# Loading the last K ahead of the last four V, and a new tail for the last batch, in a cached grouped-query attention kernel

## The chip, the cores and the metric

The kernel runs on one core of one Trainium2 chip. The metric is device time in microseconds (us), the median of several executions; it is about 2 us longer than the span of the profiled execution. A ratio is the mean time of one kernel's fast runs over the mean of the other's fast runs of the same rounds, so it is not quite the ratio of the medians that are quoted.

## The reference, cut to what matters

```python
B, Sq, D = 32, 4, 1024
Hq, Hkv, Sk, Dh = 32, 4, 2048, 128
q = (x @ wq).reshape(B, Sq, Hq, Dh).transpose(0, 2, 1, 3)
k = repeat(k_cache, 8, axis=1);  v = repeat(v_cache, 8, axis=1)   # 4 KV heads serve 32 heads
p = softmax(einsum("bhqd,bhkd->bhqk", q, k) * Dh**-0.5)
o = einsum("bhqk,bhkd->bhqd", p, v)
return o.transpose(0, 2, 1, 3).reshape(B, Sq, Hq * Dh) @ wo
```

Everything is bfloat16. Each of the 32 batches reads 2 MB of K and 2 MB of V, 134 of the 151 MB that the kernel reads. The 32 heads times 4 queries of one batch fill the 128 partitions of a score tile.

## The kernel before

The programmer places every instruction on its engine, in order, with semaphore waits. Below, `slot` hands out one of four buffers in a ring in PSUM, the memory into which this kernel's matmuls write. Names like `("pv", i)` are events. P is the exponent of the scores, P^T its transpose, o is P*V; "copied" or "evicted" means moved from PSUM to SBUF, where the kernel keeps K, V and P.

```python
def load_v(b):                       # V buffer b % 3 is free once P*V of batch b-3 is done
    ...                              # the last V comes as four loads of 512 KB, one per KV head
load_k(0); load_k(1)
for b in range(B):                   # all on one DMA queue: K2 V0 K3 V1 ... K30 V28 K31 V29 V30 V31
    if b + 2 < B:
        load_k(b + 2)
    load_v(b)
...
for i in range(B):
    pe_qk(i)                         # scores of batch i into PSUM
    softmax_max(i)                   # vector engine: one max over 2048, then the bias
    if i >= 2: pe_ot(i - 2); ot_evac(i - 2)
    if i + 1 < B:                    # transposes of K(i+1), evicted by vector and scalar engine
        for f in (0, 1): pe_fill(i + 1, f); evac(i + 1, f)
    softmax_exp(i)                   # scalar engine: P and its row sums
    if i + 1 < B:
        for f in range(2, NFILL): pe_fill(i + 1, f); evac(i + 1, f)
    softmax_rinv(i)
    if i >= 1:
        pe_pv(i - 1)                 # needs V(i-1); on the tensor engine it precedes the scores of i+1
        o_evac(i - 1)                # o / row sum
    for f in range(2): pe_pt(i, f); evac_pt(i, f)   # P^T
# ... (cut) last batch L = 31: P*V of KV heads 0-2, then of head 3; o scaled, transposed and
# copied in two parts; 128 projection matmuls; copy; output DMA
```

"P*V 28" below is `pe_pv(28)`, "scores 31" is `pe_qk(31)`, and so on.

## Time and profile before

| | before |
|---|---|
| time, median of 3 | 387.33 us (387.23 to 387.41) |
| span of the profiled execution | 385.4 us |
| one 2 MB load in the steady loop | one per 5.0 us |
| first K31 transpose / scores 31 / first P^T 31 / end of span | 358.61 / 366.13 / 371.85 / 385.4 us |

The page of the kernel before, its DMA slices and the shares of the chain that ended last:

```profile
DMA  7999999999999999999999999999999999999930
...
DMA 59%; PE 17%; ACT 13%; DVE 7%; issue 2%; SPq 1%
```

The DMA engines are busy to within two slices of the end (395 to 432 GB/s in each slice from the second to the 37th), and the chain is K loads for 59% of the span. So for most of the run nothing but bytes counts. Only the tail can change. This is its timeline (start, duration, engine, line and operation, tiles, shapes, count, then idle time and releaser, which is what ended that idle time). L207 transposes K, L240 makes scores, L248 is P*V, L225 transposes P, L296 is the projection. The first line is P*V 28, and L240 comes first for batch 30, then for 31:

```profile
354.08 1.08 PE L248 MATMUL ps_r<-V_sb,PT_sb 128*32 128x128 bf16 x64 [0.92 <-ACT KT_sb L219]
...
356.09 1.05 PE L240 MATMUL ps_s<-KT_sb,QT_sb 128*32 128x512 bf16 x16
...
358.61 2.41 PE L207 MATMUL ps_r<-ident,K_sb 128*128 128x128 bf16 x40 [1.31 <-DMA K_sb<-in_k_cache_dram]
...
364.12 1.08 PE L248 MATMUL ps_r<-V_sb,PT_sb 128*32 128x128 bf16 x64 [0.93 <-ACT KT_sb L219]
...
366.13 1.05 PE L240 MATMUL ps_s<-KT_sb,QT_sb 128*32 128x512 bf16 x16
...
367.23 2.29 DVE L280 TENSOR_REDUCE mx<-ps_s 128x1 f32<-128x2048 f32 x1 [0.15 <-PE ps_s L240]
...
369.74 1.97 ACT L285 ACTIVATE P_sb<-ps_s,negmx 128x2048 bf16<-128x2048 f32 x1 [2.09 <-DVE negmx L281]
...
371.85 1.89 PE L225 MATMUL ps_r<-ident,P_sb 128*128 128x128 bf16 x16 [1.43 <-ACT P_sb L285]
...
374.53 3.16 PE L248 MATMUL ps_r<-V_sb,PT_sb 128*32 128x128 bf16 x64 [0.68 <-DVE PT_sb L231]
...
378.18 2.80 PE L296 MATMUL ps_s<-w_sb,oT_sb 128*32 128x256 bf16 x96 [0.30 <-DVE oT_sb L364]
...
382.47 0.42 DVE L309 CAST y_sb<-ps_s 128x256 bf16<-128x256 f32 x1 [1.16 <-PE ps_s L296]
```

Read it as a chain: K31 lands (358.6), 7.5 us later come scores 31, and 19.3 us after their start the kernel ends. V31 is no part of it: its last part lands at 373.9, and P^T 31 is copied only at 374.5.

The same kernel in stretches (busy time and count of each engine, granted clock of the tensor engine, DMA share, GB/s):

```profile
367.50:370.90 3.40, 1.29 (x64) 0.97 (x64) 2.17 (x2) 1.31 (x2) 0.00 (x0) 1.00 0.51 202
370.90:377.70 6.80, 5.17 (x82) 4.71 (x82) 1.55 (x3) 1.80 (x5) 0.00 (x0) 0.50 0.17 58
```

The tensor engine worked 1.3 of 3.4 us, and in the next 6.8 us its clock was half. The DMA share is 0.5 while data is still to come. The trace has the time of each of a load's 16 completions, and they come in two halves: for V30 the eighth and the ninth are 5.7 us apart, the first and the last 9.5 us. The slow half decides when a load has landed. Landings, which I took from the trace's completions (last of 16, from the span's start):

```
        K30     then            V29     V30     V31 by KV head
before  348.5   V28 353.6  K31 358.6  363.7  368.6  370.1 371.4 372.6 373.9
after   348.4   K31 353.5  V28 358.6  363.6  368.6  369.9 371.1 372.4 373.7
```

### The profile page before, as it was taken

To read this page: it belongs to the slowest core of one execution; us is meant where nothing else is said; L and a number is where in the kernel's file an instruction comes from. 1 tells how busy PE (TensorE), PEld (TensorE's weight loads), DVE (VectorE), ACT (ScalarE), POOL (GpSimd) and SP (SyncE) were. 2 spreads that over 40 slices of the span, in tenths; PEclk is the share of its full clock that TensorE was granted. 3 is DMA by queue.
4 is the path that set the end of the run, shared out by engine and by line. 5 is a ranking of instruction groups with operands and counts; after the bars stand their busy time and mean duration, and the time that the engine had idled before them with its cause. 6 is when DMAs were issued, how large, how long until landed. Compare 5 with 4: busy or idle time off the path is not lost.

```text
span 385.4 us, 12595 instructions
## 1 busy us (share of the span) xinstructions
PE 280.9 (73%) x5929; PEld 229.5 (60%) x5929; DVE 274.1 (71%) x299; ACT 208.5 (54%) x261; POOL 0.7 (0%) x6
## 2 busy tenths in 40 slices
PE   1876888676383967888767778877767888776756
PEld 1875766465282856666655566665645676565545
DVE  0017999683552984899888859998868859987850
ACT  1005777355161646676666627766646566666620
POOL 0000000000000000000000000000000000000000
PEclk9998999886976899999999999999999999999978
DMA  7999999999999999999999999999999999999930
GB/s 328 432 432 416 418 417 398 413 410 395 413 409 409 419 416 414 419 413 418 417 419 417 417 414 417 416 416 411 417 417 417 418 420 415 417 418 410 375 143 9
DMA packets 27251, 152.32 MB, mean 395 GB/s; under 512 B 1472, under 2 KB 1984, under 8 KB 22592
## 3 DMA queue, kind: packets, MB, share of 16 engines
q1 hardware_dynamic: 27104, 151.49, 96.1%
q8 instruction: 46, 0.75, 0.8%
q10 hardware_dynamic: 96, 0.03, 0.0%
q14 instruction: 5, 0.04, 0.0%
HBM read 151.26 MB, written 0.26 MB: 393 GB/s over the span
## 4 chain that ended last, share of the span: by engine, by line
DMA 59%; PE 17%; ACT 13%; DVE 7%; issue 2%; SPq 1%
DMA K_sb<-in_k_cache_dram 59%; ACT KT_sb L219 7%; ACT P_sb L285 6%; DVE KT_sb L217 4%; PE ps_r L207 4%; PE ps_r L248 3%; PE ps_r L296 3%; PE ps_r L225 3%; PE ps_s L240 3%; DVE mx L280 2%; PE ps_s L296 1%; DVE PT_sb L231 0%; SPq L129 0%; PE ps_r L271 0%; ACT oT_sb L275 0%
## 5 line engine op out<-in xcount | busy, mean ns | idle before, releaser
L207 PE MATMUL ps_r<-ident,K_sb 128*128 128x128 bf16 x2048 | 142.6, 229 | 66.0 <-DMA K_sb<-in_k_cache_dram 40.8
L217 DVE COPY KT_sb<-ps_r 128x1024 bf16<-128x1024 bf16 x128 | 148.0, 1216 | 40.0 <-PE ps_r L207 39.8
L207 PEld LDWEIGHTS ps_r<-ident,K_sb 128*128 128x128 bf16 x2048 | 125.7, 103 | 82.2 <-DMA K_sb<-in_k_cache_dram 41.9
L219 ACT ACTIVATE KT_sb<-ps_r 128x1024 bf16<-128x1024 bf16 x128 | 124.5, 1025 | 72.1 <-PE ps_r L207 72.0
L280 DVE TENSOR_REDUCE mx<-ps_s 128x1 f32<-128x2048 f32 x32 | 73.3, 2292 | 7.1 <-PE ps_s L240 4.6
L285 ACT ACTIVATE P_sb<-ps_s,negmx 128x2048 bf16<-128x2048 f32 x32 | 63.0, 1969 | 2.2 <-DVE negmx L281 2.1
L231 DVE COPY PT_sb<-ps_r 128x1024 bf16<-128x1024 bf16 x64 | 41.4, 686 | 16.7 <-PE ps_r L225 15.2
L248 PE MATMUL ps_r<-V_sb,PT_sb 128*32 128x128 bf16 x2048 | 36.7, 223 | 17.2 <-ACT KT_sb L219 12.8
L248 PEld LDWEIGHTS ps_r<-V_sb,PT_sb 128*32 128x32 bf16 x2048 | 31.0, 98 | 22.7 <-ACT KT_sb L219 19.4
L275 ACT ACTIVATE oT_sb<-ps_r 128x128 bf16<-128x128 bf16 x31 | 8.6, 277 | 55.6 <-PE ps_r L271 55.6
L225 PE MATMUL ps_r<-ident,P_sb 128*128 128x128 bf16 x512 | 35.1, 223 | 1.8 <-ACT P_sb L285 1.4
L240 PE MATMUL ps_s<-KT_sb,QT_sb 128*32 128x512 bf16 x512 | 34.3, 386 | 2.5 <-DVE KT_sb L217 1.7
L225 PEld LDWEIGHTS ps_r<-ident,P_sb 128*128 128x128 bf16 x512 | 29.4, 99 | 5.4 <-ACT P_sb L285 1.6
L240 PEld LDWEIGHTS ps_s<-KT_sb,QT_sb 128*32 128x32 bf16 x512 | 10.8, 96 | 13.3 <-issue 2.8
L187 DVE CAST QT_sb<-ps_r 128x512 bf16<-128x512 f32 x2 | 1.3, 686 | 22.4 <-PE ps_r L176 22.4
L265 ACT ACTIVATE o_sb<-ps_r,rinv 128x128 bf16<-128x128 f32 x31 | 11.4, 367 | 9.8 <-PE ps_r L248 9.8
L189 ACT ACTIVATE QT_sb<-ps_r 128x512 bf16<-128x512 f32 x2 | 1.1, 594 | 26.0 <-PE ps_r L176 26.0
L176 PE MATMUL ps_s<-P_sb,w_sb 128*128 128x128 bf16 x128 | 9.4, 232 | 7.2 <-DMA w_sb<-in_wq_dram 7.2
L296 PE MATMUL ps_r<-w_sb,oT_sb 128*32 128x256 bf16 x384 | 11.5, 273 | 2.6 <-issue 1.4
L176 PEld LDWEIGHTS ps_s<-P_sb,w_sb 128*128 128x128 bf16 x128 | 8.3, 105 | 7.8 <-issue 4.4
L296 PEld LDWEIGHTS ps_r<-w_sb,oT_sb 128*32 128x32 bf16 x384 | 10.0, 97 | 3.7 <-issue 2.5
L271 PEld LDWEIGHTS ps_r<-ident,o_sb 128*128 128x128 bf16 x31 | 3.0, 98 | 12.7 <-issue 12.7
(30 smaller groups left out, 58.9 us busy)
## 6 DMA issues: line engine op xcount, KB each, us to landing
K_sb<-in_k_cache_dram SPq DMA_DIRECT2D x32, 2048.0 KB, 25.4
V_sb<-in_v_cache_dram SPq DMA_DIRECT2D x31, 2048.0 KB, 27.3
w_sb<-in_wq_dram SPq DMA_DIRECT2D x4, 2048.0 KB, 14.8
w_sb<-in_wo_dram SPq DMA_DIRECT2D x4, 2048.0 KB, 24.7
V_sb<-in_v_cache_dram SPq DMA_DIRECT2D x4, 512.0 KB, 15.8
P_sb<-in_x_dram SPq DMA_DIRECT2D x1, 256.0 KB, 2.8
out_dram<-y_sb SPq DMA_DIRECT2D x14, 16.0 KB, 12.1
out_dram<-y_sb ACTq DMA_DIRECT2D x2, 16.0 KB, 1.6
```

Of the source, the lines that this page charges most:

```text
L176: p.op("pe", lambda e, kt=kt, h=h: e.matmul(ps_q(h), lhsT=w_sb[:, kt, h * Dh:(h + 1) * Dh], rhs=xT_sb[:, kt, :], start=(kt == 0 and h % 4 ...
L207: p.op("pe", lambda e, q=q, t=t: e.transpose(buf[:, q * 128:(q + 1) * 128], K_sb[:, b % NKB, t, :], ident[:, :]), waits + [("k", b), "iden ...
L217: p.op("dve", lambda e: e.tensor_copy(dst, src), waits, ("kt", b, f))
L219: p.op("act", lambda e: e.activation(dst, src, ACT.Copy), waits, ("kt", b, f))
L225: p.op("pe", lambda e, q=q: e.transpose(buf[:, q * 128:(q + 1) * 128], P_sb[:, (8 * f + q) * 128:(8 * f + q + 1) * 128], ident[:, :]), wai ...
L231: p.op("dve", lambda e: e.tensor_copy(PT_sb[:, 8 * f:8 * f + 8, :].rearrange("p t q -> p (t q)"), buf), [("ptf", i, f)] + ([("pv", i - 1)] ...
L240: p.op("pe", lambda e, c=c, g=g: e.matmul(ps_s[32 * g:32 * (g + 1), c * 512:(c + 1) * 512], lhsT=QT_sb[:, i, REP * g:REP * (g + 1), :], rh ...
L248: p.op("pe", lambda e: e.matmul(buf[32 * g:32 * (g + 1), 0:Dh], lhsT=PT_sb[:, t, 32 * g:32 * (g + 1)], rhs=V_sb[:, i % NVB, g, t, :], star ...
L265: p.op("act", lambda e: e.activation(o_sb[:, :], buf[:, 0:Dh], ACT.Copy, scale=rinv[:, i:i + 1]), [("pv", i), ("rinv", i)] + ([("oT", i - ...
L280: p.op("dve", lambda e: e.tensor_reduce(mx[:, i:i + 1], ps_s[:, :], AX.X, ALU.max), [("qk", i)], ("mx", i))
L285: p.op("act", lambda e: e.activation(P_sb[:, :], ps_s[:, :], ACT.Exp, bias=negmx[:, i:i + 1], scale=scale, accum_out=ssum[:, i:i + 1]), [( ...
L296: p.op("pe", lambda e, h=h, j=j: e.matmul(buf[32 * j:32 * (j + 1), 0:NC], lhsT=oT_sb[:, h, 32 * n:32 * (n + 1)], rhs=wo_sb[:, h, NC * j:NC ...
```

## The change

The intent is to have K of the last batch early, so that its softmax is done while the last V still arrive, and then to follow V31 closely, KV head by KV head. K31 is read in 4 KB rows, so that its transposed copy is contiguous. The last max is taken in four chunks, the last exponent in two. P is normalised before it is transposed, so P*V can give o^T directly, with V as the stationary operand, and the transposes of o vanish.

```diff
 def load_k(b):
+    if b < B - 1: ...                                     # as before, 16 KB rows
+    else: src = k_cache[b].rearrange("g (p t) d -> p g (t d)", p=128)   # 4 KB rows
 for b in range(B):
-    if b + 2 < B:
+    if b + 2 < B - 1:
         load_k(b + 2)
+    if b == B - 4:
+        load_k(B - 1)               # K30 K31 V28 V29 V30 V31
     load_v(b)
 def evac(b, f):
-    if f in DVE_FILLS:
+    if f in (DVE_FILLS if b < B - 1 else (2, 3, 4, 6, 7)):
@@ last batch, cut to its core
+pe_qk(L)
+for c in range(4): mxc[c] = max(ps_s[:, c*512:(c+1)*512])          # vector engine
+mx, negmx from mxc
+pe_ot(L - 2); ot_evac(L - 2)
+for k in range(2): P[k] = exp(...), accum_out=ssum[B + k]          # scalar engine
+pe_pv(L - 1)
+ssum[L] = ssum[B] + ssum[B + 1]; softmax_rinv(L)
+for f in range(2): P[f] *= rinv (vector engine); pe_pt(L, f)
+for f in range(2): evac_pt(L, f)
+o_evac(L - 1); pe_ot(L - 1); ot_evac(L - 1)
-(P*V of heads 0-2, then 3; o scaled in two parts, transposed, copied; projection of 24 + 8 heads)
+pv_last(0)                          # 16 matmuls, lhsT = V, rhs = P^T: o^T of one KV head
+for g in range(4):
+    if g + 1 < 4: pv_last(g + 1)
+    oproj_last(g)                   # 32 projection matmuls of that head group
```

The order of the tensor engine in the loop is untouched: P*V 28 still precedes the P^T of batch 29, scores 30 and the transposes of K31.

More of the change, by code (lines that the diff above doesn't have):

```diff
@@ L111, in bass_standalone__gqa_block_cached__sampling_kernel @@
         negmx = sbuf("negmx", [128, B], F32)
-        ssum = sbuf("ssum", [128, B], F32)
+        mxc = sbuf("mxc", [128, 4], F32)
+        ssum = sbuf("ssum", [128, B + 2], F32)
         rinv = sbuf("rinv", [128, B], F32)
@@ L132, in load_k @@
         def load_k(b):
-            p.dma("sp", lambda e: e.dma_start(
-                K_sb[:, b % NKB, :, :], k_cache[b].rearrange("g (r t) d -> (g r) t d", r=R)),
+            if b < B - 1:
+                dst, src = K_sb[:, b % NKB, :, :], k_cache[b].rearrange("g (r t) d -> (g r) t d", r=R)
+            else:
+                dst = K_sb[:, b % NKB, :, :].rearrange("p (g t) d -> p g (t d)", g=G)
+                src = k_cache[b].rearrange("g (p t) d -> p g (t d)", p=128)
+            p.dma("sp", lambda e: e.dma_start(dst, src),
                 [("fill", b - NKB, NFILL - 1)] if b >= NKB else [], ("k", b), f"s_k{b % NKB}")
@@ L204, in pe_fill @@
             for q in range(TB):
-                c, v = q // (TB // C), q % (TB // C)
-                t = c * TV + f * TB // C + v
+                if b < B - 1:
+                    c, v = q // (TB // C), q % (TB // C)
+                    t = c * TV + f * TB // C + v
+                else:
+                    v, g = q // G, q % G
+                    t = g * TV + f * TB // G + v
                 p.op("pe", lambda e, q=q, t=t: e.transpose(
@@ L215, in evac @@
             src = buf.rearrange("p (c m r) -> p m r c", c=C, r=R)
-            if f in DVE_FILLS:
+            if b == B - 1:
+                dst, src = KT_sb[:, f * TB // C:(f + 1) * TB // C, :, :].rearrange("p v g m -> p (v g m)"), buf
+            if f in (DVE_FILLS if b < B - 1 else (2, 3, 4, 6, 7)):
                 p.op("dve", lambda e: e.tensor_copy(dst, src), waits, ("kt", b, f))
@@ L219, in evac, with pe_pt @@
                 p.op("act", lambda e: e.activation(dst, src, ACT.Copy), waits, ("kt", b, f))
-        def pe_pt(i, f):
+        def pe_pt(i, f, ready=None):
             buf, waits = slot(("pt", i, f))
@@ L226, in pe_pt @@
                     buf[:, q * 128:(q + 1) * 128], P_sb[:, (8 * f + q) * 128:(8 * f + q + 1) * 128], ident[:, :]),
-                    waits + [("exp", i)] if q == 0 else [], ("ptf", i, f) if q == 7 else None)
+                    waits + [ready or ("exp", i)] if q == 0 else [], ("ptf", i, f) if q == 7 else None)
         def evac_pt(i, f):
@@ L244, in pe_qk @@
                         start=True, stop=True, tile_position=(0, 32 * g)),
-                        waits, ("qk", i) if (c, g) == (3, G - 1) else None)
+                        waits, (("qk", i) if c == 3 else ("qkc", i, c)) if g == G - 1 else None)
         def pv_mm(buf, i, g, t, waits, done):
@@ L319, in bass_standalone__gqa_block_cached__sampling_kernel @@
             evac(0, f)
-        for i in range(B):
+        for i in range(B - 1):
             pe_qk(i)
@@ L346, in bass_standalone__gqa_block_cached__sampling_kernel @@
         L = B - 1
+        pe_qk(L)
+        for c in range(4):
+            p.op("dve", lambda e, c=c: e.tensor_reduce(
+                mxc[:, c:c + 1], ps_s[:, c * 512:(c + 1) * 512], AX.X, ALU.max),
+                [("qkc", L, c) if c < 3 else ("qk", L)], ("mxc", c))
+        p.op("dve", lambda e: e.tensor_reduce(mx[:, L:L + 1], mxc[:, :], AX.X, ALU.max), [("mxc", 3)], ("mx", L))
+        p.op("dve", lambda e: e.tensor_scalar(negmx[:, L:L + 1], mx[:, L:L + 1], -scale, None, op0=ALU.mult),
+             [("mx", L)], ("negmx", L))
@@ new lines, in bass_standalone__gqa_block_cached__sampling_kernel @@
+        pe_ot(L - 2)
+        ot_evac(L - 2)
+        for k in range(2):
+            p.op("act", lambda e, k=k: e.activation(
+                P_sb[:, k * 1024:(k + 1) * 1024], ps_s[:, k * 1024:(k + 1) * 1024], ACT.Exp,
+                bias=negmx[:, L:L + 1], scale=scale, accum_out=ssum[:, B + k:B + k + 1]),
+                [("negmx", L), ("ptf", L - 1, 1)], ("expk", k))
+        pe_pv(L - 1)
+        p.op("dve", lambda e: e.tensor_tensor(
+            ssum[:, L:L + 1], ssum[:, B:B + 1], ssum[:, B + 1:B + 2], op=ALU.add), [("expk", 1)], ("exp", L))
@@ L347, in bass_standalone__gqa_block_cached__sampling_kernel @@
+        softmax_rinv(L)
+        for f in range(2):
+            p.op("dve", lambda e, f=f: e.tensor_scalar(
+                P_sb[:, f * 1024:(f + 1) * 1024], P_sb[:, f * 1024:(f + 1) * 1024], rinv[:, L:L + 1], None, op0=ALU.mult),
+                [("rinv", L)], ("pn", f))
+            pe_pt(L, f, ("pn", f))
+        for f in range(2):
+            evac_pt(L, f)
+        o_evac(L - 1)
         pe_ot(L - 1)
         ot_evac(L - 1)
-        o_l, waits = slot(None)
-        waits = waits + [("pt", L, 0), ("pt", L, 1)]
@@ L351, in bass_standalone__gqa_block_cached__sampling_kernel @@
-        for t in range(TV):
-            for g in range(3):
-                pv_mm(o_l, L, g, t, waits + [("v", L, k) for k in range(3)] if t == 0 and g == 0 else [],
-                      ("pva", L) if (t, g) == (TV - 1, 2) else None)
-        for t in range(TV):
-            pv_mm(o_l, L, 3, t, [("v", L, 3)] if t == 0 else [], ("pv", L) if t == TV - 1 else None)
-        p.op("act", lambda e: e.activation(o_sb[0:96, :], o_l[0:96, 0:Dh], ACT.Copy, scale=rinv[0:96, L:L + 1]),
-             [("pva", L), ("rinv", L), ("oT", L - 1)], "oa")
@@ L359, in bass_standalone__gqa_block_cached__sampling_kernel @@
-        p.op("act", lambda e: e.activation(o_sb[96:128, :], o_l[96:128, 0:Dh], ACT.Copy, scale=rinv[96:128, L:L + 1]),
-             [("pv", L)], "ob")
-        ta, waits = slot(None)
-        ta = ta.bitcast(BF16)
-        p.op("pe", lambda e: e.transpose(ta[:, 0:96], o_sb[0:96, :], ident[0:96, 0:96]), waits + ["oa"], "oTa")
-        p.op("dve", lambda e: e.tensor_copy(
-            oT_sb[:, 0:24, L * Sq:(L + 1) * Sq], ta[:, 0:96].rearrange("p (h s) -> p h s", s=Sq)), ["oTa"], "ota")
         y_l = ps_s[:, 0:512]
@@ L367, in bass_standalone__gqa_block_cached__sampling_kernel, with pv_last @@
         n = NOG - 1
-        oproj_mm(y_l, n, range(24), ["ota", ("ot", L - 1)], None)
-        tb, waits = slot(None)
-        tb = tb.bitcast(BF16)
-        p.op("pe", lambda e: e.transpose(tb[:, 0:32], o_sb[96:128, :], ident[96:128, 96:128]), waits + ["ob"], "oTb")
-        p.op("dve", lambda e: e.tensor_copy(
-            oT_sb[:, 24:32, L * Sq:(L + 1) * Sq], tb[:, 0:32].rearrange("p (h s) -> p h s", s=Sq)), ["oTb"], "otb")
-        oproj_mm(y_l, n, range(24, 32), ["otb"], ("op", n))
+        def pv_last(g):
+            buf, waits = slot(None)
+            for t in range(TV):
+                p.op("pe", lambda e, t=t: e.matmul(
+                    buf[:, 0:32], lhsT=V_sb[:, L % NVB, g, t, :], rhs=PT_sb[:, t, 32 * g:32 * (g + 1)],
+                    start=(t == 0), stop=(t == TV - 1)),
+                    waits + [("v", L, g), ("pt", L, 0), ("pt", L, 1)] if t == 0 else [],
+                    ("pvl", g) if t == TV - 1 else None)
+            p.op("dve", lambda e: e.tensor_copy(
+                oT_sb[:, 8 * g:8 * (g + 1), L * Sq:(L + 1) * Sq], buf[:, 0:32].rearrange("p (h s) -> p h s", s=Sq)),
+                [("pvl", g)], ("otl", g))
@@ L375, in bass_standalone__gqa_block_cached__sampling_kernel, with oproj_last @@
+        def oproj_last(g):
+            oproj_mm(y_l, n, range(8 * g, 8 * (g + 1)), [("otl", g), ("ot", L - 1), ("exp", L)],
+                     ("op", n) if g == G - 1 else None)
+        pv_last(0)
+        for g in range(G):
+            if g + 1 < G:
+                pv_last(g + 1)
+            oproj_last(g)
         oproj_evac(y_l, n)
```

## The prediction

> **What bounds the kernel.** The slices of the page show DMA at 9 tenths almost to the end and about 417 GB/s; the chain of waits is 59% K loads. From the landings in the trace, one 2 MB load lands every 5.0 us: K30 348.5, V28 353.6, K31 358.6, V29 363.7, V30 368.6, the four parts of V31 at 370.1, 371.4, 372.6, 373.9 us of a 385.4 us span. Half of each load's 16 completions come up to 10 us before the other half (the windows after 364 us show a DMA share of 0.5), so the slow half sets every landing and stays backlogged; a later issue does not delay it. [...]
>
> The steady loop is DMA-bound: the early iterations, whose K was already there, took 8.65 us from score matmul to score matmul, against 10.0 us of data. So only the tail after 353 us can change. There, by the chain: K31 lands 358.6, scores of batch 31 begin 366.1, max 367.2 to 369.5, exponent to 371.8, transposes to 373.8 and P*V at half clock to 377.7, projection to 382.5, end 385.4. V31 (373.9) is hardly waited for.
>
> **What the change does.** Bytes are unchanged. K31 lands one place earlier (353.6), but V28 takes its place: 358.6 in place of 353.6. P*V of batch 28 began at 354.1 before. On the tensor engine it stands, in order, ahead of scores 30 and of the transposes of K31; so the early K31 cannot be used before V28 lands. Tensor engine idle from 353.2 to 358.6.
>
> New walk, with traced durations: P*V 28 from 358.6, 1.08 us, transposes 1.0, scores 30 1.0: 361.7 with a full clock. After 5.4 us idle I expect half clock ([...] here the clock was 0.5 from 370.9 to 377.8 after a nearly idle window, and 64 P*V took 3.16 in place of 1.08 us, 16 transposes 1.89 in place of 1.07). That adds about 3 us: scores 30 end near 365. Batch 31's K eviction is cheaper (1216 to about 690 ns each on the vector engine, as the equally shaped P^T copies): about 0.9 us off the 7.65 us from scores to scores. Scores 31 begin near 371.7 (368.5 if no throttle) against 366.1.
>
> Tail from there: four max chunks, estimated 0.69 us each from the 2048- and 256-column operations, run after the P^T copies: no gain on 2.29 us. Two exponents with accumulator reads 2.4 against 2.07 us; sum, reciprocal and normalisation about 0.7 more on the path. P^T starts 7.3 us after scores against 5.7, again after about 5 us idle, so at half clock. Then 64 P*V matmuls with full-width V weights (about 62 ns each, 118 throttled) replace 64 small ones, the transposes of o vanish, and 128 projection matmuls stay: about 9 us against 8. Output 2.5 us as before. Tail about 22.5 us against 19.3.
>
> Sum: 3 to 6 us later scores, 3 us longer tail: +6 to +9 us, nearly all on the critical path.
>
> **Predicted: 394.5 us**, range 390.5 to 398. Faster by over 2%: 0.02; within 2%: 0.54; slower by over 2%: 0.44.
>
> **What the profile would show.** P*V 28 waiting on DMA of V for about 4.5 us; clock 0.5 near 357 to 364 and again near 378; scores 31 later than 366; no wait for V31; data ending near 374; eviction near 690 ns.
>
> **What would make it wrong.** No throttle in either gap (then about 390); a slow normalisation; a different skew of the DMA halves on that chip; V28 landing early enough to hide its delay.

The sum: 3 to 6 us later scores and a tail longer by 3 us, +6 to +9 us, and a point of 394.5 us. The half clock is the estimate from one measured stretch, 370.9 to 377.7 us of the kernel before. That a later issue does not delay a landing was an inference, and the changed kernel bears it out: V28 was issued at 334.11 us, 1.19 us later than K31 before, and landed at 358.60 against 358.56; the parts of V31 were issued 3.9 to 5.5 us later than before and landed 0.24 to 0.27 us earlier. The 2.4 us for two exponents and the 0.7 us for sum, reciprocal and normalisation are estimates; the changed kernel took 2.31 us (374.29 to 376.60) and 0.91 us (376.60 to 377.51).

## The result, and the profile after

The changed kernel takes 391.99 us (391.98 to 392.75, 3 runs) against 387.33 us; ratio 1.0127, 95% interval 1.0104 to 1.015. That is slower, but within 2%. Its timeline (L261 is P*V, L238 the transposes of P, L253 scores, L218 transposes of K, L362 the max chunks, L371 the exponents, L380 the normalisation, L395 the last P*V, L309 the projection):

```profile
358.73 1.90 PE L261 MATMUL ps_r<-V_sb,PT_sb 128*32 128x128 bf16 x64 [4.93 <-DMA V_sb<-in_v_cache_dram]
...
360.56 1.89 PE L238 MATMUL ps_r<-ident,P_sb 128*128 128x128 bf16 x16
...
362.38 1.56 PE L253 MATMUL ps_s<-KT_sb,QT_sb 128*32 128x512 bf16 x16
...
363.94 2.40 PE L218 MATMUL ps_r<-ident,K_sb 128*128 128x128 bf16 x40
...
368.32 1.08 PE L261 MATMUL ps_r<-V_sb,PT_sb 128*32 128x128 bf16 x64
...
370.53 1.05 PE L253 MATMUL ps_s<-KT_sb,QT_sb 128*32 128x512 bf16 x16
371.40 2.47 DVE L362 TENSOR_REDUCE mxc<-ps_s 128x1 f32<-128x512 f32 x4
...
374.29 1.11 ACT L371 ACTIVATE P_sb<-ps_s,negmx 128x1024 bf16<-128x1024 f32 x1 [2.23 <-DVE negmx L366]
...
377.01 0.88 DVE L380 TENSOR_SCALAR P_sb<-P_sb,rinv 128x1024 bf16<-128x1024 bf16 x2
...
377.56 1.89 PE L238 MATMUL ps_r<-ident,P_sb 128*128 128x128 bf16 x16 [3.00 <-DVE P_sb L380]
...
380.32 1.02 PE L395 MATMUL ps_r<-PT_sb,V_sb 128*128 128x32 bf16 x32 [0.77 <-DVE PT_sb L244]
...
381.27 1.90 PE L309 MATMUL ps_s<-w_sb,oT_sb 128*32 128x256 bf16 x32
...
385.25 1.93 PE L309 MATMUL ps_s<-w_sb,oT_sb 128*32 128x256 bf16 x64
...
387.23 0.42 DVE L322 CAST y_sb<-ps_s 128x256 bf16<-128x256 f32 x1 [1.69 <-PE ps_s L309]
```

P*V 28 begins at 358.73, 0.13 us after V28 landed, where it began at 354.08 before. The waits of the stretch from 353 us on name the releaser (waiter, releaser, total us, times, longest), and the stretches show the clock:

```profile
PE ps_r L261 <- DMA V_sb<-in_v_cache_dram: 4.9, 1, 4.9
```

```profile
353.20:358.70 5.50, 0.60 (x10) 0.42 (x7) 1.85 (x3) 1.59 (x2) 0.00 (x0) 0.81 1.03 411
358.70:363.50 4.80, 4.77 (x92) 3.73 (x96) 1.38 (x2) 0.37 (x1) 0.00 (x0) 0.50 0.77 299
...
377.10:383.90 6.80, 5.57 (x105) 4.46 (x109) 2.72 (x7) 0.28 (x1) 0.00 (x0) 0.50 0.00 0
```

The tensor engine is busy 0.6 of 5.5 us before V28, and its clock is half when it resumes. It is half again in the tail. All of the difference of the two spans (390.18 - 385.43 = 4.75 us) is found by subtracting starts in the two timelines:

| stretch | before | after | difference |
|---|---|---|---|
| P*V 28 begins | 354.08 | 358.73 | +4.65 |
| from there to scores 30 | 2.01 | 3.65 | +1.64 |
| scores 30 to scores 31 | 10.04 | 8.15 | -1.89 |
| scores 31 to first P^T 31 | 5.72 | 7.03 | +1.31 |
| first P^T 31 to the last copy | 10.62 | 9.67 | -0.95 |
| last copy to the end | 2.96 | 2.95 | -0.01 |

So the new tail as a whole (the last three lines) is +0.35 us. The loss is that V28 landed in K31's old place.

### The profile page after: what moved, and what is told of

Read it like the earlier page. It is cut to its first block, busy times and chain, and to the rows that moved or that the text cites. A ratio compares the mean times of both kernels' runs of the same rounds, so it can differ in the third digit from the quotient of the medians.

```text
span 390.2 us, 12599 instructions
## 1 busy us (share of the span) xinstructions
PE 282.3 (72%) x5927; PEld 230.2 (59%) x5927; DVE 274.1 (70%) x309; ACT 207.0 (53%) x260; POOL 0.7 (0%) x6
## 4 chain that ended last, share of the span: by engine, by line
DMA 58%; PE 16%; ACT 12%; DVE 10%; issue 2%; SPq 1%
DMA K_sb<-in_k_cache_dram 52%; DMA V_sb<-in_v_cache_dram 6%; ACT KT_sb L232 6%; ACT P_sb L298 5%; DVE KT_sb L230 5%; PE ps_r L218 3%; PE ps_r L238 3%; DVE mx L293 3%; PE ps_r L309 3%; PE ps_s L253 3%; PE ps_r L261 2%; PE ps_s L309 1%; DVE PT_sb L244 1%; DVE mxc L362 1%; ACT P_sb L371 1%
## 5 line engine op out<-in xcount | busy, mean ns | idle before, releaser
L218 PE MATMUL ps_r<-ident,K_sb 128*128 128x128 bf16 x2048 | 142.3, 229 | 64.4 <-DMA K_sb<-in_k_cache_dram 39.6
L230 DVE COPY KT_sb<-ps_r 128x1024 bf16<-128x1024 bf16 x129 | 146.5, 1196 | 39.0 <-PE ps_r L218 38.9
L218 PEld LDWEIGHTS ps_r<-ident,K_sb 128*128 128x128 bf16 x2048 | 125.3, 103 | 80.2 <-DMA K_sb<-in_k_cache_dram 40.5
L293 DVE TENSOR_REDUCE mx<-ps_s 128x1 f32<-128x2048 f32 x31 | 71.0, 2292 | 7.2 <-PE ps_s L253 5.6
L298 ACT ACTIVATE P_sb<-ps_s,negmx 128x2048 bf16<-128x2048 f32 x31 | 61.0, 1969 | 0.1
L261 PE MATMUL ps_r<-V_sb,PT_sb 128*32 128x128 bf16 x1984 | 34.4, 223 | 19.8 <-ACT KT_sb L232 11.9
L261 PEld LDWEIGHTS ps_r<-V_sb,PT_sb 128*32 128x32 bf16 x1984 | 28.8, 98 | 24.9 <-ACT KT_sb L232 17.5
L238 PE MATMUL ps_r<-ident,P_sb 128*128 128x128 bf16 x512 | 35.9, 225 | 3.3 <-DVE P_sb L380 3.0
L253 PE MATMUL ps_s<-KT_sb,QT_sb 128*32 128x512 bf16 x512 | 34.4, 386 | 2.7 <-DVE KT_sb L230 1.7
L238 PEld LDWEIGHTS ps_r<-ident,P_sb 128*128 128x128 bf16 x512 | 30.2, 101 | 7.1 <-DVE P_sb L380 3.2
L253 PEld LDWEIGHTS ps_s<-KT_sb,QT_sb 128*32 128x32 bf16 x512 | 10.9, 96 | 13.9 <-issue 3.4
L309 PE MATMUL ps_r<-w_sb,oT_sb 128*32 128x256 bf16 x384 | 11.5, 273 | 3.1 <-issue 1.9
L309 PEld LDWEIGHTS ps_r<-w_sb,oT_sb 128*32 128x32 bf16 x384 | 10.0, 97 | 4.2 <-issue 3.0
```

The lines of the kernel that those rows point to most:

```text
L218: p.op("pe", lambda e, q=q, t=t: e.transpose(buf[:, q * 128:(q + 1) * 128], K_sb[:, b % NKB, t, :], ident[:, :]), waits + [("k", b), "iden ...
L230: p.op("dve", lambda e: e.tensor_copy(dst, src), waits, ("kt", b, f))
L238: p.op("pe", lambda e, q=q: e.transpose(buf[:, q * 128:(q + 1) * 128], P_sb[:, (8 * f + q) * 128:(8 * f + q + 1) * 128], ident[:, :]), wai ...
L253: p.op("pe", lambda e, c=c, g=g: e.matmul(ps_s[32 * g:32 * (g + 1), c * 512:(c + 1) * 512], lhsT=QT_sb[:, i, REP * g:REP * (g + 1), :], rh ...
L261: p.op("pe", lambda e: e.matmul(buf[32 * g:32 * (g + 1), 0:Dh], lhsT=PT_sb[:, t, 32 * g:32 * (g + 1)], rhs=V_sb[:, i % NVB, g, t, :], star ...
L293: p.op("dve", lambda e: e.tensor_reduce(mx[:, i:i + 1], ps_s[:, :], AX.X, ALU.max), [("qk", i)], ("mx", i))
```

## The experiments

Theory A: the order of the loads does the harm. P*V 28 stands on an in-order engine ahead of scores 30, so an earlier K31 can't be used before V28 has come. Then the idle engine loses its clock (0.50 in the stretch above). Rival B: the new tail does the harm, and the order costs nothing. The first four kernels run on one chip, beside the kernel before (387.11 us, 7 runs).

### e1: the order alone

```diff
 # kernel before
-    if b + 2 < B:
+    if b + 2 < B - 1:
         load_k(b + 2)
+    if b == B - 4:
+        load_k(B - 1)
```

> The kernel before with one edit: K31 is loaded ahead of V28 (still in 16 KB rows), old tail. Theory A (V28 lands where K31 did, and P*V 28 stands in the tensor engine's order ahead of scores 30, so the engine stalls about 4.7 us and then runs at half clock): +4.65 us of wait, +1.6 us of half clock, -1.4 us because K31 is no longer waited for; about 392.2 us. Rival B (the order costs nothing; the new softmax chunks, the normalisation of P and the full-width V weights make the tail longer): about 387.3 us.

Measured: 391.83 us (4 runs), ratio 1.0125 (1.0105 to 1.0144). With the old tail, the old rows and one line moved, the whole loss is there. The timeline of e1 has the same wait:

```profile
358.59 1.54 PE L250 MATMUL ps_r<-V_sb,PT_sb 128*32 128x128 bf16 x64 [4.66 <-DMA V_sb<-in_v_cache_dram]
...
370.78 1.05 PE L242 MATMUL ps_s<-KT_sb,QT_sb 128*32 128x512 bf16 x16
```

Scores 31 begin at 370.78, and 19.3 us later (390.1) the kernel ends, as before. B falls. As e1 and the changed kernel are equal in time, everything else in the change sums to about zero while the order stands.

### e2: the order undone

```diff
 # changed kernel
-    if b + 2 < B - 1:
+    if b + 2 < B:
         load_k(b + 2)
-    if b == B - 4:
-        load_k(B - 1)
```

> The changed kernel with one edit: K31 is loaded behind V28 again (4 KB rows and the new tail kept). Theory A: scores 31 begin near 365.2 us in the trace (366.1 before, less 0.9 for the cheaper K evictions), tail 19.7 us as in the changed kernel; about 386.8 us. Rival B: about 391.5 to 392 us.

Measured: 388.06 us (4 runs), ratio 1.003 (1.0011 to 1.0048). The loss is nearly gone, but not as fully as A said. Two terms were off, and the trace has both:

```profile
363.90 1.08 PE L259 MATMUL ps_r<-V_sb,PT_sb 128*32 128x128 bf16 x64 [1.01 <-DVE rinv L301]
...
365.91 1.05 PE L251 MATMUL ps_s<-KT_sb,QT_sb 128*32 128x512 bf16 x16
...
372.93 1.89 PE L236 MATMUL ps_r<-ident,P_sb 128*128 128x128 bf16 x16 [2.57 <-DVE P_sb L378]
...
379.00 1.90 PE L307 MATMUL ps_s<-w_sb,oT_sb 128*32 128x256 bf16 x32
```

First, scores 31 came at 365.91, not 365.2. The wait of P*V 29 (first line) is put down to a reciprocal of the vector engine, which it does not need. V29 landed at 363.76, 0.14 us before its start, the same gap as at P*V 28 above. So cheaper K evictions bring little here (scores 31 0.2 us earlier than the 366.13 of the kernel before), because the V behind K31 is the next limit. Second, the clock was half for 10.2 us in the tail (370.6 to 380.8), where it was 6.8 us in the changed kernel: the second projection group still took 1.90 us (last line). Span less scores 31 is 20.4 us.

### e3: the clock in the gap

```diff
 def pe_pv(i):
     buf, waits = slot(("o", i)); ...
+    if i == B - 4:
+        for m in range(60):         # identity times identity, into a corner of buf that nothing reads
+            matmul(buf[:, 384:512], lhsT=ident, rhs=ident)
```

> The changed kernel with 60 matmuls of the identity put ahead of P*V 28, into an unused corner of its PSUM buffer, so that the tensor engine is busy while it waits for V28. If the half clock costs what the trace suggests (P*V 28 1.90 in place of 1.08 us, transposes 1.89 in place of 1.07, scores 30 1.56 in place of 1.05), scores 31 come 1.6 us earlier: about 390.4 us. If the clock plays no part: 392.0 us. If the extra matmuls themselves run at half clock they last 6.4 us and delay P*V 28: 393 us.

Measured: 390.47 us (4 runs), ratio 1.009 (1.0074 to 1.0106).

```profile
353.94 3.52 PE L269 MATMUL ps_r<-ident 128*128 128x128 bf16 x60
...
358.67 1.08 PE L261 MATMUL ps_r<-V_sb,PT_sb 128*32 128x128 bf16 x64 [1.21 <-DMA V_sb<-in_v_cache_dram]
...
359.68 1.07 PE L238 MATMUL ps_r<-ident,P_sb 128*128 128x128 bf16 x16
...
368.32 1.05 PE L253 MATMUL ps_s<-KT_sb,QT_sb 128*32 128x512 bf16 x16
```

P*V 28 is back at 1.08 us, and scores 31 come at 368.32, 2.21 us earlier than in the changed kernel. The wait itself remained. From P*V 28 to scores 30 it is 2.01 us again (3.65 in the changed kernel), and scores 30 themselves take 1.05 in place of 1.56 us. So the half clock in this gap cost 1.64 + 0.51, about 2.1 us. The time came out 1.5 us lower, because this run's tail had half clock for 10.2 us (372.9 to 383.1) and is 0.7 us longer (20.32 against 19.65 us). So the close match with the expected 390.4 us is in part luck: more was gained in the gap than expected, and the excess was lost in the tail.

### e4: the blocking taken away

The loads stay as in the change. P*V 28 goes behind scores 30, P*V 29 behind scores 31, and P^T gets a second buffer, so nothing has to wait that did not before.

```diff
-PT_sb = sbuf("PT_sb", [128, TV, 128], BF16)
+PT_sb = sbuf("PT_sb", [128, 2, TV, 128], BF16)      # batch i uses half i % 2
-    if i >= 1:
+    if 1 <= i < B - 3:
         pe_pv(i - 1); o_evac(i - 1)
+    if i == B - 2:
+        pe_pv(i - 2); o_evac(i - 2)
 # last batch: pe_pv(29) behind scores 31, then pe_pv(30)
```

> The changed kernel with K31 early as it is, but P*V 28 and 29 placed one batch later in the tensor engine's order (behind scores 30 and 31), with a second P^T buffer. Theory A (the harm is the order of the engine, not that V28 lands late): no stall at P*V 28, scores 31 near 363.5 us, tail 19.7 us, so about 385 us, faster than both. Rival (late data bounds the end however the engine is ordered, or another engine's queue holds scores 31): 390 us or more.

Measured: 386.0 us (4 runs), ratio 0.9975 (0.9955 to 0.9996), and correct.

```profile
360.21 1.08 PE L261 MATMUL ps_r<-V_sb,PT_sb 128*32 128x128 bf16 x64
...
362.42 1.05 PE L253 MATMUL ps_s<-KT_sb,QT_sb 128*32 128x512 bf16 x16
...
368.83 1.90 PE L261 MATMUL ps_r<-V_sb,PT_sb 128*32 128x128 bf16 x64 [0.78 <-DMA V_sb<-in_v_cache_dram]
```

V28 lands as late as in the change (358.5), but scores 31 now begin at 362.42, 8.1 us earlier. So the late V28 hurts only through the order of the engine. Of these 8.1 us, only 6.6 reach the span (383.6 against 390.2): the tail is 21.2 us here, with half clock from 367.5 to 377.7 us, and with the o of batch 29 evicted between the two exponents, which set the second one back by 1.0 us.

### e5 and e6: the clock in both tails

The next four ran beside the kernel before at 387.28 us (7 runs). A filler is a matmul whose result nothing reads.

```diff
 # e5: in kernel e2;  e6: in the kernel before
 def pe_pv(i):
+    if i == B - 2: 25 matmuls of the identity, ahead of P*V 30
 ...
+28 (e6) or 38 (e5) matmuls of the identity behind P*V 30, in a ring slot of their own
```

> The changed kernel with K31 behind V28 again, and 25 + 38 matmuls of the identity put around P*V 30 so that the tensor engine stays busy up to the last transposes of P. Against that kernel without them (388.06 us, half clock from 370.6 to 380.8 us): transposes 1.89 to 1.07 us and the first two projection groups 1.90 to about 0.95 us each, so 2.7 us less, about 385.4 us. If the half clock were not what makes this tail 20.4 us, no gain.

> The kernel before with nothing but the same idle filling (25 + 28 matmuls of the identity around P*V 30). Transposes 1.89 to 1.07 us, last P*V 3.16 to 1.08 us: 2.9 us less, about 384.2 to 384.4 us. Read against e5: with the clock taken out of both, the new tail with old load order should be no better than the old one (about 1 us worse, for the chunks and the normalisation on the path). If the new tail is better at full clock, e5 comes out below e6.

Measured: e5 385.66 us (4 runs), ratio 0.9964 (0.9949 to 0.998); e6 386.02 us (4 runs), ratio 0.9972 (0.9953 to 0.9991). In both, the clock stayed full to the end of the work. In e5 the first transposes of P 31 take 1.09 in place of 1.89 us (in e6 1.06):

```profile
372.90 1.09 PE L236 MATMUL ps_r<-ident,P_sb 128*128 128x128 bf16 x16
```

At full clock and with the old order, the new tail is as good as the old one, not a microsecond worse; the intervals overlap. e5 came out near what was expected (385.4 us). e6 gained 1.3 us in place of 2.9, and this showed an error in the walk:

```profile
374.04 1.05 PE L248 MATMUL ps_r<-V_sb,PT_sb 128*32 128x128 bf16 x46 [0.93 <-PE ps_r L279]
...
375.29 1.07 PE L248 MATMUL ps_r<-V_sb,PT_sb 128*32 128x128 bf16 x18 [0.20 <-issue]
```

The last P*V of the kernel before is not one group of four interleaved KV heads like the others, but three interleaved heads and then the fourth. In the trace, a step of several interleaved heads starts every 0.055 us at full clock and every 0.107 us at half clock, one head or four. So this P*V has 32 steps in e6 and 28 in the kernel before, in place of 16: at half clock it takes 1.7 times as long as P*V 28 (3.16 against 1.90 us). Reading its 3.16 us as the time of any P*V at half clock was wrong. Two smaller losses add to e6's shortfall: the fillers, the last of which starts near 371.9 us, held the first P^T 31 back by 0.36 us (6.08 us behind scores 31, against 5.72), and P*V 31 pauses after its 46th matmul (0.42 us from start to start). Without these two, e6 would be some 0.7 us faster, so e5 and e6 tell the two tails apart no better than that.

### e7: early K31 without blocking, at full clock

Kernel e4, with the last max and exponent whole, the last transposes ahead of P*V 30, and fillers behind the transpose of o 29:

```diff
 pe_qk(L); softmax_max(L)
 pe_ot(L - 3); ot_evac(L - 3)
 pe_pv(L - 2); o_evac(L - 2); pe_ot(L - 2); ot_evac(L - 2)
+56 matmuls of the identity
 softmax_exp(L); softmax_rinv(L)
 normalise P and pe_pt(L, 0), (L, 1); evac_pt(L, 0), (L, 1)
 pe_pv(L - 1); o_evac(L - 1)
 pv_last(0); pe_ot(L - 1); ot_evac(L - 1); ...       # the rest as in the change
```

> The kernel e4 (K31 early, P*V 28 and 29 one batch later) with the max and the exponent of the last batch whole again, the last transposes ahead of P*V 30, and 56 matmuls of the identity in the idle time. Transposes of P 31 near 369 us at full clock, P^T ready near 371, then P*V and projection by head group following V31 (370.1 to 373.9 us): end near 380 us in the trace, about 382 us, faster than both kernels. If V31 or something else bounds the end, 384 us or more.

Measured: 384.85 us (4 runs), ratio 0.9947 (0.9925 to 0.9969). It beats both kernels, but by less than expected. P^T 31 began at 368.88 as expected. Then this, in the first projection group (L315):

```profile
368.88 1.07 PE L238 MATMUL ps_r<-ident,P_sb 128*128 128x128 bf16 x16 [0.33 <-DVE P_sb L381]
...
372.12 0.51 PE L315 MATMUL ps_s<-w_sb,oT_sb 128*32 128x256 bf16 x11
373.89 0.83 PE L315 MATMUL ps_s<-w_sb,oT_sb 128*32 128x256 bf16 x21 [1.27 <-issue]
```

The group stops after 11 of its 32 equal matmuls, for 1.27 us, without a releaser ("issue").

### e8: the chunks alone

```diff
 # changed kernel
-four max chunks and their max; two exponents and the sum of their sums
+softmax_max(L); softmax_exp(L)
```

> The changed kernel with the last max and the last exponent whole again (one operation each, no sum of two parts); the normalisation of P and the rest kept. The chunks' trace shows max, exponent and sum done 6.3 us after scores 31 begin, against 5.7 us in the kernel before: 0.5 us less expected, about 391.5 us. If chunking helps, slower than 392.0 us.

Measured: 391.84 us (4 runs), ratio 1.0123 (1.01 to 1.0146): not told apart from the changed kernel by its time. In its trace, the stretch from scores 31 to the first P^T is 6.44 us against 7.03 us:

```profile
371.08 1.05 PE L253 MATMUL ps_s<-KT_sb,QT_sb 128*32 128x512 bf16 x16
...
377.52 1.38 PE L238 MATMUL ps_r<-ident,P_sb 128*128 128x128 bf16 x16 [2.01 <-DVE P_sb L368]
```

So in the trace the chunks cost 0.6 us of path and gain nothing. But scores 31 came 0.55 us later in this execution, because its half clock around P*V 28 came 1 us later (357.6 to 364.5 us, against 356.6 to 363.5). So where the stretch of half clock lay made about half a microsecond of difference between these two executions.

### e9 and e10: the pause in e7

Theory F for the pause: the engine is out of instructions, which come to it in blocks of 256. What speaks for it are counts in the traces. The queue that the page calls "instruction" moved 46 packets of 16 KB in the kernel before, and every matmul is two instructions with its weight load (5929 of each). In the kernel before, P*V 30 pauses in the same way after 53 of its 64 matmuls (off the path). Counted from the start, the same number of matmuls, 5707, is reached in e7 at the 53rd filler; from there to the pause there are 3 fillers, 16 transposes, 64 of P*V 30, 16 + 1 + 16 of o and 11 of the projection, together 127, so 254 instructions, and the trace has two semaphore waits of the tensor engine among them: 256. (The expectation of e9 says 128 matmuls; it left the waits out.) And a packet of the instruction queue ended 1.26 us before the pause did (1.43 and 1.52 us before the end of the pause in P*V 30 in the kernel before and in the changed one). These two ran on one chip beside the kernel before at 386.30 us (11 runs).

```diff
 # e9: in e7
-56 matmuls of the identity, 128 columns each
+14 matmuls, 512 columns each
 # e10: in e9, besides
+50 matmuls of the identity ahead of P*V 8        # more work, where the loop waits for data
```

> The kernel e7 with its 56 short filler matmuls replaced by 14 of 512 columns (same time, 84 instructions fewer). Theory F: the 1.27 us pause inside projection group 0 of e7 (no releaser in the profile) is the tensor engine out of instructions at a block of 256 (128 matmuls with their weight loads): it lies just 128 matmuls behind the pause of the kernel before in P*V 30, and an instruction fetch of 16 KB ends 1.3 us ahead of its end. Then the pauses move: one to about the 22nd matmul of P*V 30, the next to about the 5th of projection group 1; time 384 to 386 us. Rival: the pause is a wait for data or for a slot; it stays at the 12th matmul of projection group 0.

> The kernel e9 with 50 more short matmuls of the identity ahead of P*V 8, where the loop waits for data anyway: more work, later code unchanged. Theory F: block ends move 50 matmuls earlier in the code, to the 2nd filler and to about the 3rd matmul of projection group 0; the block in between now lasts about 6.5 us, longer than the 5.6 us from a block's start to the use of the next one in e7, so there is no pause on the path: about 1.3 us less than e7, 383.3 to 383.8 us. Rival: no difference from e9.

Measured: e9 383.48 us (6 runs), ratio 0.9922 (0.9909 to 0.9936); e10 383.14 us (6 runs), ratio 0.9906 (0.9888 to 0.9924).

```profile
374.60 0.39 PE L315 MATMUL ps_s<-w_sb,oT_sb 128*32 128x256 bf16 x5
...
375.21 0.94 PE L315 MATMUL ps_s<-w_sb,oT_sb 128*32 128x256 bf16 x27 [0.22 <-issue]
```

```profile
365.77 0.59 PE L269 MATMUL ps_r<-w_sb,ident 128*128 128x512 bf16 x2
...
366.63 2.53 PE L269 MATMUL ps_r<-w_sb,ident 128*128 128x512 bf16 x11 [0.28 <-issue]
...
372.40 1.45 PE L320 MATMUL ps_s<-w_sb,oT_sb 128*32 128x256 bf16 x32
```

In e9 the pause is in projection group 1 after the 5th matmul, the place that F named, and none is left in group 0. In e10 it moves, with unchanged code in the tail, to the 2nd filler in the trace (which has 13 of the 14) and into group 0, where the matmul starts of the trace have a hole of 0.41 us behind the third. So the place is shown: it follows the count of instructions and not the data. What the engine does in the pause, no trace shows.

The traces of the other runs show it too. Counted from the start of each, two for a matmul and one for a semaphore wait, the pause in P*V 30 comes after instruction 11457 in the kernel before, the changed kernel, e1, e2, e5, e6 and e8 alike (in e5 and e6, with 25 fillers ahead, after the 28th matmul and not the 53rd), and the pauses of e6 in P*V 31 and of e7 after 11713, which is 256 more. The counts of e9 and e10 are two and three lower, for a matmul or a wait missing from their traces. The traces of e3 and e4 show no such pause in the tail.

The lengths were not foretold. From matmul start to matmul start, where the others of such a group are at most about 0.1 us apart, it is 1.54 us in e7, 0.49 us in e9, and 0.41 us in e10, where I had expected none; and there is no pause at all in P*V 30 of e9. What sets the length (the load on the DMA engines, or how long the block before lasts) stays open. e9 and e10 are not told apart in time. Either beats both kernels, by 0.8 to 0.9% against the kernel before. The interval of e9 overlaps that of e7, which ran on another chip, so the time does not show that e9 is faster than e7. And no run has P*V late with the old load order: how much of the gain of e4, e7, e9 and e10 needs K31 early is not shown.

## Why the prediction was right

The prediction was 394.5 us with a range of 390.5 to 398.0; the result is 391.99. It was right in sign, range and class (within 2% was the likeliest, at 0.54), and 2.5 us too high. Part of this is luck. The walk itself is 4.0 us too high: its scores 31 at 371.7 and its tail of 22.5 us end at 394.2 us of span, and 390.18 was measured. The sum "+6 to +9 us" does not hold the +4.66 us that were measured. The point was set lower than the walk, and the range reached down to a case without throttle, which is not what happened.

- **DMA order, right.** V28 was to land at 358.6 and did (358.60). P*V 28 waited 4.9 us. e1 shows that this alone makes the loss, and e4 that it does so through the order of the engine.
- **Half clock in both gaps, right in kind, too large in size.** "64 P*V took 3.16 in place of 1.08 us" was the term that was mis-sized: P*V 28 took 1.90. The 3.16 us belong to the P*V of three heads and then one. "That adds about 3 us" (to the end of scores 30) is about 2.1 us, as e3 shows by taking it away.
- **Cheaper K evictions, right in size.** About 690 ns each were predicted on the vector engine, and they took 681 ns. 0.9 us was predicted between scores 30 and 31. From e1 (8.90 us) to e3 (7.64 us) it is 1.26 us, of which 0.25 us is e1's half clock in scores 30 (1.30 against 1.05 us), so about 1.0. e2 shows that under the old order they are worth little.
- **Scores 31 near 371.7:** measured 370.53, from the P*V term.
- **Chunks no gain, right.** Max chunks 2.47 us against 2.29; P^T 7.03 us behind scores against 7.3 predicted and 5.72 before. e8 shows 0.6 us of it to be chunking.
- **Tail +3 us, wrong in size: +0.35 us.** The step that failed is "64 P*V matmuls with full-width V weights (about 62 ns each, 118 throttled)". In the trace they start 27 ns apart at half clock (1.02 us for the first 32) and 25 ns apart at full clock (0.57 us for the last 16). P*V and projection, put at about 9 us against 8, took 6.91 us (380.32 to 387.23) against 7.94: that is 2.1 of the 2.85 us by which the predicted tail was too long. I had taken the pace of transposes with 128 moving columns (16 in 1.0 and in 1.89 us; their starts are 56 ns apart at full clock and 107 ns at half); these have 32. The exact reason for their pace was not tried.
- **V31 not waited for, right.** The intent was to end on V31. It landed at 373.66, but P^T 31 was ready only at 380.2. In e7, e9 and e10 the two meet, near 371 to 374 us, and there the head-grouped P*V may be worth having; no run tries those kernels without it.

## What to carry to other kernels

Before moving a load earlier, list the load that it displaces, and find the first instruction on each in-order engine that needs that one. An early operand is worth nothing if its consumer stands behind another wait. A gap on the tensor engine can cost its length and then again in clock (here 4.65 us, and then about 2.1 us, which e3 took away), so compare kernels with equal clock before judging a tail. A duration should only be borrowed for another instruction group if that one interleaves the same way and moves as many columns (here 3.16 us of another interleaving stood for 1.90, and 62 and 118 ns of 128 columns for 25 and 27 ns of 32).

## What the traces show besides

- P*V 28 of the changed kernel started 0.13 us after the sixteenth completion of V28 (358.60), and 5.5 us after the eighth (353.23). Half of the completions fell behind more and more: in the kernel before, the ninth came 0.4 us after the eighth for V4, which landed near 97 us, and 5.7 us after it for V30, and the DMA share was near 0.5 from 367 to 372 us. Why is open.
- Half clock did not need an idle engine: a stretch with the engine busy for 1.3 of 3.4 us was followed by it (before, 367.5 to 370.9 us). In the traces of the kernel before and the changed kernel, the stretches at half clock, but for the last, which the end of the trace cuts off, are 3.41, 6.83 or 10.24 us long. Counted in pieces of 3.41 us from 30 us on, in these two traces: at full clock, each of the 14 pieces with up to 1.43 us of busy time was followed by half clock, and none of the 168 with 1.69 us or more (ends of matmuls are modelled in the traces). At half clock, each of the 12 pieces with up to 2.60 us was followed by half clock again, and each of the 13 with 3.22 us or more by full. These are counts, not a rule; no run was made to find the limits.
- At the place of the pause, two matmul starts were 0.41 to 1.54 us apart on the critical path (e10, e9, e7), and 1.81 us off it (P*V 30 after the change; 0.64 us before it).
